# Diagonal term of stages 4 to 7 by GpSimd, the spread of w by two matmuls side by side, and the prologue listed anew

## The chip, the core and the metric

The kernel runs on one core of a Trainium2 chip. A core has TensorE (PE; weight loads are shown apart as PEld), VectorE (DVE), ScalarE (ACT), GpSimd (POOL) and SyncE (SP), and 16 DMA engines that serve the queues of POOL, ACT and SP. The metric is the device time of one execution in microseconds (us), lower being better. The kernel before takes 170.57 us, the median of 3 runs from 170.1 to 171.39.

## What is computed

A linear attention with a decaying state, whose result goes through two matrix products with a leaky ReLU between them. The inputs r, k, v have 4 batches, 8 heads, 768 tokens and 48 channels a head; w and u have one value per head and channel.

```python
for t in range(S):
    cur = np.einsum('bhd,bhe->bhde', u[None] * kt, vt)
    y[:, :, t] = np.einsum('bhd,bhde->bhe', rt, state + cur)
    state = w[None, :, :, None] * state + np.einsum('bhd,bhe->bhde', kt, vt)
...
x = attn_out.transpose(0, 2, 1, 3).reshape(B * S, H * D)   # 3072 x 384
h = x @ w_in                                               # 384 x 2048
out = np.maximum(0.01 * h, h) @ w_out                      # 2048 x 384
```

The diagonal term is `cur`: what a token's own k and v give to its own y. For head h it is v of the token times the sum over the channels of r, u and k.

## The kernel before

The 768 tokens of each batch are cut into 6 chunks of 128; the 24 pairs of chunk and batch are called stages, numbered chunk first, so that stages 0 to 3 are the first chunk of the four batches, and stage n continues the state of stage n-4. For one stage:

- P (`prep_half`, L344, VectorE): r and k are multiplied by tables of powers of w (qtab, ktab), which gives q and k scaled to the middle of the chunk, in the tile qk. They need the loads of r and k.
- T and t (`turn_mm`, L398, and `turn_out`): qk is turned (channels to partitions) by four matmuls with the identity, and copied from PSUM into tp. Stages 0 to 7 do it so; from stage 8 on, X (`turn_dma`, L349) does it by a DMA transpose on the queue of SP.
- A (`a_mm`, L423): eight matmuls, two per pair of heads, of 48 rows each, alternately on the upper and lower rows of the array, give the scores of token against token in two PSUM banks.
- M (`a_mask_half`, halves a and b): VectorE brings the scores into the tile at, with the strict triangle alone.
- The diagonal term, in one of two ways. For n < DIAG: X (`diag`, L359) multiplies the turned q and k, D (`diag_mm`, L451) sums them over channels with the weights w u by four matmuls of two columns, Q (`scaled_v`, L366) multiplies v by the sums, and Y begins with three matmuls of the identity (L550) that put it into PSUM; M is a product with the mask (L432). For n >= DIAG: q (`row_sums`, L373, L375, L377, VectorE) computes k u, r k u and its sum over channels from the loaded r and k; Q (`diag_tile`, L384, GpSimd, two instructions) writes the identity times these sums into at; M is a predicated copy (L436) that writes the scores over it where the mask is set, and Y needs no further matmul.
- Y (`y_mm`, L557): the state and the scores against v, in strips of 32 columns: 16 small matmuls for stages 0 to 3, 28 for others. y (`y_out`, L571, ScalarE) copies the sum into xT.
- K and S (`kv_mm`, L464, and `state`): k transposed times v, and the new state: for stages from 4 on a sum (L525) and a product (L527).
- G, g or J, j (`g1`, L596, one stage with one group of 512 columns of w_in; `g1_pair`, L619, two stages with 256 columns; ScalarE's leaky ReLU behind each) and H, h (`g2`, L643, output copy L655, output DMA L657).
- r, k, v, wi, wo are loads on the queue of GpSimd (L222, L232, L236), in the order listed; r0 and k0 alone go by SP and ACT.
- F (`fill`, L260): matmuls of ones into a free bank, whose result nothing reads; the number is how many, of 256 columns each.

The order of the work up to stage 5's outputs is a written list, ORDER (L27 to L38), of such tokens with their stage. Every engine executes its part of the list in that order; semaphore waits come from which tile an operation reads and writes. After the list a regular loop (L696) over pairs of stages follows, from the pair 6 and 7 on: first matmuls of the pair, row sums and diagonal tiles of the pair after it, loads three pairs ahead, second matmuls, scores, Y, masks, states. The last of the list on TensorE are Y7, A9 and A8.

The tables come from w in the beginning: w is loaded as a row on one partition, spread over 128 partitions by a matmul with a row of ones (`spread_w`, L295, half of the channels at a time, in float32), its logarithm taken (lnw, L301) and the powers by an exponential (L306), each in halves A and B. Cm, Wl, C and W make columns of w and w u for the state and the diagonal sums; u16, U and utab spread u.

## Time and profile before

| | |
|---|---|
| median of 3 runs | 170.57 us |
| profiled execution | 170.54 us |
| its span, first to last instruction | 168.8 us |
| TensorE busy | 164.0 us, 97% of the span |
| VectorE, ScalarE, GpSimd busy | 107.6, 92.5, 103.8 us |
| share of the chain that ended last on TensorE | 96% |
| of it second matmuls (L643), first matmuls of pairs (L619) | 37%, 31% |
| fills (L260), 26 matmuls | 6.8 us busy, 2% of the chain |
| diagonal products on GpSimd (L384), 32 | 35.0 us, 1.12 each |
| GpSimd's queue (software DMA) | 10.03 MB in 76512 packets |

A line of a timeline has the start in us from the beginning of the span, the time from the start of the first to the end of the last of the instructions that it joins, the engine, the line of the kernel, the operation, what it writes and reads, and their number; in brackets the idle time before it and what ended that. Matmuls overlap their neighbours, so the difference of two starts tells what one costs, and it is less than the time shown. POOL's DMA lines are the issuing; the data lands some microseconds later.

### The profile page before, as it was taken

How to read it: one execution, taken by the hardware profiler on the slowest of the kernel's cores; microseconds unless marked ns; L12 is line 12 of the kernel's file. 1: busy time of each engine (PE TensorE's matmuls, PEld its weight loads, DVE VectorE, ACT ScalarE, POOL GpSimd, SP SyncE). 2: the span in 40 equal slices, each digit the busy share in tenths (PEclk: the TensorE clock that was granted, in tenths of full speed). 3: DMA queues.
4: the chain of work that ended last, by engine and by line, in shares of the span. 5: the costliest groups of instructions: out<-in, count | busy, mean ns of one | idle time of the engine just before them, and what ended most of it. 6: DMA issues, size and time to landing. Idle time of an engine off the chain costs nothing.

```text
span 168.8 us, 4933 instructions
## 1 busy us (share of the span) xinstructions
PE 164.0 (97%) x2127; PEld 124.4 (74%) x2127; DVE 107.6 (64%) x215; ACT 92.5 (55%) x172; POOL 103.8 (61%) x117
## 2 busy tenths in 40 slices
PE   5999999899999999999999999999999999999994
PEld 3577899798667867867867867768768668668663
DVE  7379989884376999999859959969866050000000
ACT  3855899587123933933834835735637538449221
POOL 7999999990059979897993993993707200000000
PEclk9999999999999999999999999999999999999999
DMA  6999999999999999969999299299941011011022
GB/s 106 155 170 133 163 163 173 185 190 149 110 177 144 161 62 153 193 82 169 126 140 171 55 143 177 65 109 131 147 122 50 0 50 47 0 50 47 25 74 93
DMA packets 99146, 19.67 MB, mean 117 GB/s; under 512 B 92338, under 2 KB 99124, under 8 KB 99124
## 3 DMA queue, kind: packets, MB, share of 16 engines
q0 software_dynamic: 76512, 10.03, 93.1%
q1 hardware_dynamic: 21554, 9.12, 25.2%
q8 instruction: 17, 0.28, 0.6%
q10 hardware_dynamic: 1058, 0.20, 0.6%
q14 instruction: 5, 0.04, 0.1%
HBM read 20.45 MB, written 4.72 MB: 149 GB/s over the span
## 4 chain that ended last, share of the span: by engine, by line
PE 96%; DVE 1%; issue 1%; ACT 0%; DVEq 0%
PE ps L643 37%; PE ps L619 31%; PE ps L596 6%; PE ps L557 6%; PE ps L423 4%; PE ps L260 2%; PE ps L464 2%; PE ps L398 2%; PE ps L295 1%; PE ps L550 1%; DVE v_sb L280 1%; PE ps L451 1%; PE ps L321 0%; DVE qk L344 0%; ACT out_sb L655 0%
## 5 line engine op out<-in xcount | busy, mean ns | idle before, releaser
L643 PE MATMUL ps<-w_out_sb,gT 128*128 128x384 bf16 (+2 forms) x400 | 65.7, 320 | 0.0
L619 PE MATMUL ps<-xT,w_in_sb 128*128 128x256 bf16 x480 | 54.3, 273 | 0.0
L643 PEld LDWEIGHTS ps<-w_out_sb,gT 128*128 128x128 bf16 x400 | 37.9, 98 | 22.1
L619 PEld LDWEIGHTS ps<-xT,w_in_sb 128*128 128x128 bf16 x480 | 46.7, 98 | 6.5 <-ACT xT L571 0.2
L384 POOL TENSOR_TENSOR at<-ident,s_tok 128x512 bf16<-128x512 bf16 x32 | 35.0, 1121 | 26.8 <-DVE s_tok L377 26.8
L629 ACT ACTIVATE gT<-ps 128x512 bf16<-128x512 f32 x80 | 47.8, 597 | 6.2 <-PE ps L619 1.3
L655 ACT ACTIVATE out_sb<-ps 128x384 f32<-128x384 f32 (+2 forms) x25 | 11.9, 477 | 52.9 <-PE ps L643 52.9
L436 DVE CAST_PREDICATED at<-mask,ps 128x512 bf16<-128x512 uint16 x32 | 19.9, 684 | 15.5 <-PE ps L423 15.5
L222 POOL DMA_DIRECT2D v_sb<-in_v_dram x24 | 22.5, 953 | 0.0
L222 POOL DMA_DIRECT2D k_sb<-in_k_dram x23 | 21.6, 947 | 0.0
L222 POOL DMA_DIRECT2D r_sb<-in_r_dram x23 | 21.1, 943 | 0.0
L571 ACT ACTIVATE xT<-ps 128x384 bf16<-128x384 f32 x24 | 11.0, 492 | 6.5 <-PE ps L557 6.5
L344 DVE TENSOR_TENSOR qk<-r_sb,qtab 128x384 bf16<-128x384 bf16 x23 | 13.4, 592 | 1.9 <-DMA r_sb<-in_r_dram 1.9
L344 DVE TENSOR_TENSOR qk<-k_sb,ktab 128x384 bf16<-128x384 bf16 x23 | 13.9, 606 | 0.0
L375 DVE TENSOR_TENSOR rku<-r_sb,ku 128x384 bf16<-128x384 bf16 x16 | 12.7, 794 | 0.5
L525 DVE TENSOR_TENSOR sum_t<-ps,st 128x384 bf16<-128x384 f32 x16 | 8.8, 550 | 5.2 <-PE ps L464 5.2
L596 PE MATMUL ps<-xT,w_in_sb 128*128 128x128 bf16 x192 | 12.0, 219 | 0.0
L557 PE MATMUL ps<-at,v_sb 128*32 128x128 bf16 x384 | 11.1, 219 | 0.6 <-issue 0.6
L432 DVE TENSOR_TENSOR at<-ps,mask 128x512 bf16<-128x512 f32 x16 | 10.5, 682 | 0.9 <-PE ps L423 0.9
L606 ACT ACTIVATE gT<-ps 128x512 bf16<-128x512 f32 x16 | 9.6, 600 | 2.7 <-PE ps L596 2.1
L596 PEld LDWEIGHTS ps<-xT,w_in_sb 128*128 128x128 bf16 x192 | 10.9, 98 | 0.1
L557 PEld LDWEIGHTS ps<-at,v_sb 128*32 128x32 bf16 x384 | 8.7, 97 | 1.1 <-issue 0.7
(60 smaller groups left out, 131.7 us busy)
## 6 DMA issues: line engine op xcount, KB each, us to landing
out_dram<-out_sb SPq DMA_DIRECT2D x23, 192.0 KB, 3.9
v_sb<-in_v_dram POOLq DMA_DIRECT2D x24, 96.0 KB, 6.0
r_sb<-in_r_dram POOLq DMA_DIRECT2D x23, 96.0 KB, 5.6
k_sb<-in_k_dram POOLq DMA_DIRECT2D x23, 96.0 KB, 5.1
w_in_sb<-in_moe_w_in_dram POOLq DMA_DIRECT2D x4, 384.0 KB, 5.6
w_out_sb<-in_moe_w_out_dram POOLq DMA_DIRECT2D x4, 384.0 KB, 7.9
tp<-qk SPq DMA_TRANSPOSE x16, 4.6
k_f<-in_k_dram ACTq DMA_DIRECT2D x1, 192.0 KB, 2.8
```

The costliest lines, as they stand in the source:

```text
L222: add("pool", lambda: G.dma_start(dst, src), R=pace, W=[(which, n)], dma=f"{which}{n}")
L344: add("dve", lambda: V.tensor_tensor(qk[iq][:, H * half:H * half + H, 0:D], hd(src), hd(tab[:, :]), ALU.mult), R=[(name, n), ("qk"[half] + ...
L375: add("dve", lambda: V.tensor_tensor(rku[i2][:, :], r_of(n), ku[i2][:, :], ALU.mult), R=[("r", n), ("ku", i2)], W=[("rku", i2)])
L384: add("pool", lambda hh=hh, s_of=s_of: G.tensor_tensor(at[ia][:, hh, :, :], ident[:, :].unsqueeze(1).to_broadcast([128, NP, 128]), s_of.un ...
L436: add("dve", lambda: V.copy_predicated(at[n % NAT][:, hh, :, :], mask[:, :].bitcast(mybir.dt.uint16).unsqueeze(1).to_broadcast([128, NP, 1 ...
L557: last = PE.matmul(ps_y[32 * q:32 * q + 32, 128 * s:128 * s + 128], a, m, start=not whole and step == 0, stop=step == len(columns[q]) - 1)
L571: add("act", lambda: A.activation(xT[m % NX][:, :, 128 * half:128 * half + 128], ps_y[:, 0:HD].rearrange("p (s t) -> p s t", t=128), AF.Copy),
L596: last = PE.matmul(ps_g[:, 128 * f:128 * f + 128], w_in_sb[:, s, 128 * fb:128 * fb + 128], xT[ix][:, s, t], start=s == 0, stop=s == NSL - 1)
L619: last = PE.matmul(ps_g[:, 256 * f:256 * f + 256], w_in_sb[:, s, 128 * fb:128 * fb + 128], xT[ix][:, s, :], start=s == 0, stop=s == NSL - 1)
L629: add("act", lambda: A.activation(gT[ig][:, 2 * j:2 * j + 2, :].rearrange("p f t -> p (f t)"), ps_g[:, :], AF.Prelu, alpha=0.01), R=[key], ...
L643: last = PE.matmul(ps_o[:, 0:c1 - c0], gT[ig][:, s, 128 * half:128 * half + 128], w_out_sb[:, s, c0:c1], start=s == 0, stop=s == NFB - 1)
L655: add("act", lambda: A.activation(out_sb[io][:, c0:c1], ps_o[:, 0:c1 - c0], AF.Copy), R=[key], W=held)
```

## The change

DIAG goes from 8 to 4. So stages 4 to 7 take the second way for the diagonal term: row sums on VectorE, the diagonal tile by two products on GpSimd for each stage, and a predicated copy for the mask; their X, D and the three matmuls of Y with the identity are gone.

w is loaded as two rows of 192, on partitions 0 and 64, and spread by two matmuls, one on each partition, into two neighbouring PSUM banks; logarithm and tables are then one instruction of 384 columns each instead of two of 192. For that the eight banks become one tensor, and one_row has 128 partitions. u8 and u are loaded by SP instead of ACT. A fill has 128 columns instead of 256.

The whole list is written anew. Among the moves: the memsets of qk stand ahead of ones; r2 is GpSimd's first load and wi1 the second; stage 2's q is made first; fills are 76 of 128 columns in 21 places instead of 26 of 256 in 9; Q4 and Q5 stand after the load of k6, Q7, Q6, Q9 and Q8 among and behind the last loads; the transposes of stages 9 and 8 (X9T, X8T) come after P9q and P8q, and the list ends on TensorE with K9, Y7, Y6, A9, A8. On VectorE the last part reads S8, M7b, M7a, M6b, S7, P10k, M6a, S9, P11k, M9a. Lines of the changed kernel are 1 to 9 higher than before: L353 is `prep_half`, L393 the diagonal product, L441 and L445 the two forms of the mask, L559 and L566 those of Y.

```diff
--- before.py
+++ after.py
@@ -23,18 +23,18 @@
 NSL = HD // 128
 
 FIRST, NB, PACE = 6, B, 3
-TURNED, DIAG, CARRY, EXACT = 8, 8, 4, 1
+TURNED, DIAG, CARRY, EXACT = 8, 4, 4, 1
 ORDER = """
-w k0 r0 u8 w8 u ones tcol wi0 v0z r2 table exps one id wlz qk0 F6 bcA r1 id8 F2 bcB lnA k1 u16 wu8 ktabA F1 Cm k2 lnB U
-qtabA ktabB v0 utab P0k qtabB Wl wi3 F6 T0k P0q W C tri t0k@ F1 T0q v1 P1q t0q P2q F6 T1q X0 r3 A0 P1k t1q T2q M0a T1k
-k3 t2q D0 P2k F1 K0 t1k Q0 T2k v2 M0b t2k F1 A1 X1 v5 F2 Y0 X2 M1b A2 k4 y0 D2 M1a D1 K1 G0.0 k5 Q1 M2b G0.3 g0.0 wi1
-P3q Y1 P3k g0.3 r4 S1 T3q y1 K2 Q2 T3k t3q v3 G1.3 S2 t3k M2a G1.0 r5 g1.3 P4k Y2 X3 g1.0 r8 P5k A3 S0 y2 K5 M3b r6 T5k
-G2.3 t5k S5 k7 G2.0 g2.3 M3a G1.1 k9 g2.0 P4q G0.1 g1.1 wi2 T4k g0.1 D3 P5q K3 r7 T4q Q3 t4k T5q G2.1 S3 t5q k6 P8q Y3
-t4q P6q X5 A5 v4 g2.1 P7k A4 X4 y3 D5 T6q M4a wo3 T7k t6q G3.0 M5a v8 t7k G3.3 Q5 g3.0 wo0 M5b D4 G3.1 g3.3 P9k k8 G2.2
-M4b g3.1 P7q G1.2 wo2 g2.2 P6k T7q v6 g1.2 T6k t7q@ K4 Y5 t6k Q4 wo1 A7 y5 X6 A6 k11 S4 Y4 M7b v9 D6 y4 G3.2 M6a v10
-J2.4 M6b g3.2 J2.3 M7a v11 j2.4 J2.5 X7 j2.3 r10 D7 J2.1 j2.5 q8 r9 J2.2 j2.1 J2.6 r11 j2.2 P8k J2.0 j2.6 v7 X8T K8 Q6
-K6 j2.0 G0.2 k10 S6 Y6 g0.2 S8 J2.7 y6 H1 j2.7 P11k K9 H2 h1 S9 P10q H0 h2 P9q q9 X9T P11q K7 Q9 H3 Q7 h0 X11T S7 P10k
-X10T Q8 Y7 h3 A9 y7 A8 M9a M8a M9b M8b k12 r12 v12 k13 r13 v13
+w k0 r0 w8 u8 u qk0 r2 table ones wi1 one v0z id F12 bc tcol r1 exps id8 wlz lnw k3 qtab wu8 v0 F10 Cm u16 P2q ktab P0q
+F2 U r3 T2q Wl P0k utab T0q k1 C t2q T0k t0q k2 t0k@ W P1q tri F9 A0 X0 wi3 P3k F1 T1q M0b v3 F3 K0 M0a t1q F2 T3k F3
+D0 wi2 P3q t3k S0 F6 T3q v2 Q0 t3q P2k F12 Y0 P1k k4 X3 A3 y0 F1 T1k r5 M3b F1 D3 T2k t1k G0.1 M3a t2k v1 G0.3 X1 g0.1
+Q3 r4 D1 K3 X2 g0.3 A1 S3 F1 A2 r7 Y3 M1a F1 D2 M1b k5 y3 F3 G0.2 M2a G3.3 wo0 g0.2 Q2 G3.1 wi0 P4k g3.3 M2b T4k g3.1
+G3.2 v5 P5q t4k Q1 K1 T5q wo3 g3.2 Y2 S1 P4q t5q Y1 v4 q4 y2 F2 T4q y1 v10 F2 G2.1 t4q G1.2 k6 g2.1 P5k P7q G2.2 g1.2
+q5 Q4 T5k g2.2 G1.1 t5k T7q G2.3 g1.1 t7q Q5 A5 F1 A4 g2.3 G3.0 M4a F1 G1.0 M4b g3.0 K5 wo1 G0.0 M5a g1.0 r6 M5b G2.0
+g0.0 S5 K2 k9 Y5 g2.0 S2 F1 Y4 y5 k7 K4 y4 F2 G1.3 S4 wo2 J2.4 g1.3 P6k r9 J2.7 j2.4 T6k r10 j2.7 J2.6 t6k J2.3 q6 v7
+j2.6 J2.1 j2.3 k8 J2.0 j2.1 v11 P9k J2.2 P7k j2.0 P6q T7k r8 q7 j2.2 J2.5 t7k T6q v8 H1 j2.5 t6q r11 q9 v6 k10 P10q A7
+h1 P8k A6 P9q H2 Q7 X9T q8 v9 P11q K8 H3 h2 P8q Q6 S8 X8T M7b M7a k11 K6 M6b K7 h3 H0 Q9 S7 P10k Q8 M6a K9 X10T Y7 h0
+S9 Y6 y7 A9 y6 A8 P11k M9a X11T M9b M8b M8a S6 k12 r12 v12 k13 r13 v13
 """
 
 
@@ -148,9 +148,9 @@
     r_sb = SB("r_sb", [128, NST, HD])
     k_sb = SB("k_sb", [128, NST, HD])
     v_sb = SB("v_sb", [128, NST, H * E])
-    w_row = SB("w_row", [1, HD], FP32)
+    w_row = SB("w_row", [128, HD // 2], FP32)
     u_row = SB("u_row", [1, HD], FP32)
-    one_row = SB("one_row", [1, 128], FP32)
+    one_row = SB("one_row", [128, 128], FP32)
     u_row16 = SB("u_row16", [1, HD])
     w_head = SB("w_head", [H, D], FP32)
     u_head = SB("u_head", [H, D], FP32)
@@ -169,7 +169,7 @@
     kexp = SB("kexp", [128, 1], FP32)
     wcol = SB("wcol", [128, NP], FP32)
     wl = SB("wl", [128, NP, 2 * D])
-    ones = SB("ones", [128, 256])
+    ones = SB("ones", [128, 128])
     mask = SB("mask", [128, 128])
     ident = SB("ident", [128, 128])
     ku = [SB(f"ku{i}", [128, HD]) for i in range(4)]
@@ -184,7 +184,8 @@
     xT = [SB(f"xT{i}", [128, NSL, 256]) for i in range(NX)]
     gT = [SB(f"gT{i}", [128, NFB, 256]) for i in range(NG)]
     out_sb = [SB(f"out_sb{i}", [128, HD], FP32) for i in range(NO)]
-    ps = [ctx.enter_context(nc.psum_tensor(f"ps{i}", [128, 512], FP32)) for i in range(8)]
+    ps_all = ctx.enter_context(nc.psum_tensor("ps", [128, 8, 512], FP32))
+    ps = [ps_all[:, i, :] for i in range(8)]
 
     V, A, PE, SP, G = nc.vector, nc.scalar, nc.tensor, nc.sync, nc.gpsimd
     sch = Sched(ctx, nc)
@@ -257,7 +258,7 @@
 
         def emit():
             for _ in range(n):
-                last = PE.matmul(ps[i][:, 0:256], ones[:, 0:128], ones[:, 0:256], start=True, stop=True)
+                last = PE.matmul(ps[i][:, 0:128], ones[:, :], ones[:, :], start=True, stop=True)
             return last
 
         add("pe", emit, R=["ones"], W=[("ps", i), f"fill{n}"])
@@ -287,24 +288,32 @@
         add("dve", lambda: V.memset(wl[:, :, :], 0.0), W=["wl"])
         add("dve", lambda: V.memset(wu[:, :, :], 0.0), W=["wu"])
 
-    half_bank = {}
-
-    def spread_w(half):
-        ps_w, key = half_bank[half] = take()
-        cols = slice(192 * half, 192 * half + 192)
-        add("pe", lambda: PE.matmul(ps_w[:, cols], one_row[:, :], w_row[:, cols], start=True, stop=True),
-            R=["one_row", "w_row"], W=[key])
-
-    def log_w(half):
-        ps_w, key = half_bank[half]
-        cols = slice(192 * half, 192 * half + 192)
-        add("act", lambda: A.activation(lnw[:, cols], ps_w[:, cols], AF.Ln), R=[key], W=[("lnw", half)])
-        give(key)
-
-    def table(dst, exps, name, half):
-        cols = slice(192 * half, 192 * half + 192)
-        add("act", lambda: A.activation(dst[:, cols], lnw[:, cols], AF.Exp, scale=exps[:, 0:1]),
-            R=[("lnw", half), name + "exp"], W=[(name + "tab", half)])
+    w_bank = []
+
+    def spread_w():
+        for half in range(2):
+            w_bank.append(take())
+        assert w_bank[1][1][1] == w_bank[0][1][1] + 1
+
+        def emit():
+            for half in range(2):
+                at0 = slice(64 * half, 64 * half + 1)
+                last = PE.matmul(w_bank[half][0][:, 0:192], one_row[at0, :], w_row[at0, :], start=True, stop=True)
+            return last
+
+        add("pe", emit, R=["one_row", "w_row"], W=[w_bank[0][1], w_bank[1][1]])
+
+    def log_w():
+        i = w_bank[0][1][1]
+        add("act", lambda: A.activation(lnw[:, :].rearrange("p (two c) -> p two c", two=2),
+                                        ps_all[:, i:i + 2, 0:192], AF.Ln),
+            R=[w_bank[0][1], w_bank[1][1]], W=["lnw"])
+        give(w_bank[0][1])
+        give(w_bank[1][1])
+
+    def table(dst, exps, name):
+        add("act", lambda: A.activation(dst[:, :], lnw[:, :], AF.Exp, scale=exps[:, 0:1]),
+            R=["lnw", name + "exp"], W=[name + "tab"])
 
     def small_identity():
         add("dve", lambda: V.tensor_copy(ident8[:, :], ident[0:H, 0:H]), R=["ident"], W=["ident8"])
@@ -342,7 +351,7 @@
         iq = n % NQK
         src, tab, name, done = ((r_of(n), qtab, "r", "qp"), (k_of(n), ktab, "k", "kp"))[half]
         add("dve", lambda: V.tensor_tensor(qk[iq][:, H * half:H * half + H, 0:D], hd(src), hd(tab[:, :]), ALU.mult),
-            R=[(name, n), ("qk"[half] + "tab", 0), ("qk"[half] + "tab", 1), ("qk0", iq)], W=[(done, iq)])
+            R=[(name, n), "qk"[half] + "tab", ("qk0", iq)], W=[(done, iq)])
 
     def turn_dma(n):
         iq = n % NQK
@@ -659,16 +668,16 @@
 
     half_of = {"q": 0, "k": 1, "a": 0, "b": 1}
     single = {
-        "w": lambda: add("sp", lambda: SP.dma_start(w_row[:, :], row(w)), W=["w_row"], dma="w"),
+        "w": lambda: add("sp", lambda: SP.dma_start(
+            w_row[0:65:64, :], dram(w, 0, [[HD // 2, 2], [1, HD // 2]])),
+            W=["w_row"], dma="w"),
         "w8": lambda: add("sp", lambda: SP.dma_start(w_head[:, :], by_head(w)), W=["w_head"], dma="w8"),
-        "u8": lambda: add("act", lambda: A.dma_start(u_head[:, :], by_head(u)), W=["u_head"], dma="u8"),
-        "u": lambda: add("act", lambda: A.dma_start(u_row[:, :], row(u)), W=["u_row"], dma="u"),
+        "u8": lambda: add("sp", lambda: SP.dma_start(u_head[:, :], by_head(u)), W=["u_head"], dma="u8"),
+        "u": lambda: add("sp", lambda: SP.dma_start(u_row[:, :], row(u)), W=["u_row"], dma="u"),
         "one": lambda: add("dve", lambda: V.memset(one_row[:, :], 1.0), W=["one_row"]),
         "tcol": tokens, "ones": filled, "exps": exponents, "v0z": zero_v, "qk0": zero_qk, "wlz": zero_w,
         "id": identity, "tri": triangle, "table": preload, "id8": small_identity, "wu8": wu_product,
-        "bcA": lambda: spread_w(0), "bcB": lambda: spread_w(1), "lnA": lambda: log_w(0), "lnB": lambda: log_w(1),
-        "qtabA": lambda: table(qtab, qexp, "q", 0), "qtabB": lambda: table(qtab, qexp, "q", 1),
-        "ktabA": lambda: table(ktab, kexp, "k", 0), "ktabB": lambda: table(ktab, kexp, "k", 1),
+        "bc": spread_w, "lnw": log_w, "qtab": lambda: table(qtab, qexp, "q"), "ktab": lambda: table(ktab, kexp, "k"),
         "Cm": columns_mm, "Wl": log_columns, "C": decay_columns, "W": decay_table,
         "u16": u_cast, "U": u_spread, "utab": u_table,
     }
```

## The prediction

> **What bounds the kernel now.** I read the page first, then the chain that ended last, then the timelines of each engine up to 63 us.
>
> ```profile
> span 168.8 us, 4933 instructions
> PE 164.0 (97%) x2127; PEld 124.4 (74%) x2127; DVE 107.6 (64%) x215; ACT 92.5 (55%) x172; POOL 103.8 (61%) x117
> PE 96%; DVE 1%; issue 1%; ACT 0%; DVEq 0%
> ```
>
> The chain is TensorE nearly from end to end. From 53.52 us on, where the written list ends and the regular loop begins, both kernels do the same work in the same order. So the question is when the loop's first pair of matmuls (L619) can start, and whether its feeding engines are late by then. In the trace of before:
>
> ```profile
> 9.03 1.49 PE L260 MATMUL ps<-ones 128*128 128x256 bf16 x6
> 12.61 0.40 PE L398 MATMUL ps<-ident,qk 128*128 128x128 bf16 x4 [0.18 <-DVE qk L344]
> 31.94 0.23 PE L557 MATMUL ps<-at,v_sb 128*32 128x128 bf16 x2 [0.56 <-issue]
> 53.52 5.41 PE L619 MATMUL ps<-xT,w_in_sb 128*128 128x256 bf16 x48
> ```
>
> Between 12.8 and 53.5 TensorE pauses once, for 0.56 us at 31.4, with no releaser. Everything else is work. The other engines have room late in the prologue: GpSimd waits 10.22 us before stage 9's diagonal tiles, and VectorE is busy 5.31 of the 10 us from 40 to 50.
>
> The rows that decide this change are VectorE's and GpSimd's when both work on SBUF:
>
> ```profile
> 48.53 4.28 POOL L384 TENSOR_TENSOR at<-ident,s_tok 128x512 bf16<-128x512 bf16 x4 [10.22 <-DVE s_tok L377]
> 47.43 0.36 DVE L375 TENSOR_TENSOR rku<-r_sb,ku 128x384 bf16<-128x384 bf16 x1
> 50.71 1.19 DVE L344 TENSOR_TENSOR qk<-k_sb,ktab 128x384 bf16<-128x384 bf16 x1
> 57.39 2.97 DVE L375 TENSOR_TENSOR rku<-r_sb,ku 128x384 bf16<-128x384 bf16 x1
> 69.38 1.08 DVE L375 TENSOR_TENSOR rku<-r_sb,ku 128x384 bf16<-128x384 bf16 x1
> ```
>
> A VectorE product of two SBUF tiles takes 0.35 us alone; one that meets a GpSimd diagonal product (1.05 each) ends 0.2 us after that product ends. Products that read PSUM (L366 at 48.55, L525 at 49.69) keep their 0.55 beside the same tiles.
>
> **Part by part.** All terms are against the profiled execution: 170.54 us, a span of 168.8 and 1.74 around it; the median of the runs is 170.57. I laid the two lists out engine by engine, each instruction starting when its engine is free and what it waits for has ended, with start-to-start durations from the rows. For before this gives 52.7 for the loop's first matmul; the trace has 53.52, of which 0.56 is the pause without releaser.
>
> *TensorE's own work.* In before, from the first turning matmul (7.96) to 53.52, the rows give: turning 4.5, A 3.3, D 1.0, K 2.05, Y 6.3, first matmuls 10.7 and 5.25, second 10.4, fills 2.1, together 45.6. Removed: four groups D of 0.105, 0.4; three 128-column matmuls (L550) in each of Y4 to Y7, whose groups go from 0.77 to the 0.45 of the loop's Y, 1.3. The pause and short waits before D, A and K, some 1.4 with it, need not recur. Added: fills after that point are 52 of 128 columns, 18 at 0.107 and 34 at 0.056, 3.8 in place of 2.1. The first turning matmul moves to 6.6 (next part). So 6.6 + 45.6 - 0.4 - 1.3 - 1.4 + 1.7 gives 50.8: 2.7 us early if nothing waits.
>
> *The start.* ones and one_row come behind six memsets of 0.14, so the fills begin at 2.0 instead of 1.25, end at 3.3 and cover nothing that was needed before. The spread of w: each half took 0.92 (L295); side by side I take 0.92 for both, at most 1.84. Nearest row: A's eight matmuls of 48 rows, alternating between upper and lower rows, take 0.26, 33 ns each, against 56 ns in turning. Then log 0.49 and one table of 384 columns instead of two of 192 (0.35 to 0.45 each; I take 0.60, bounds 0.44 and 0.9), u's cast 0.43, the second table 0.60: ktab ends at 6.65, stage 0's k product at 7.24, its turn at 8.04. qtab alone, at 5.4, releases stage 2's q, whose load is now first on POOL's queue (5.1). w8, u8 and u now all queue behind r0 on SP; by w8's row (1.67 to 4.56) they land at 4.6, 5.1 and 5.6, and the cast of u waits 0.1.
>
> *VectorE.* The first masks move from 11.6 to 9.6. From 8.1 on it is never long idle: 12.2 us of products up to stage 4's row sums and 1.1 of waits puts these at 21.3. Per stage 4 to 7 it loses prod 0.33 and scaled v 0.46, and gains ku, rku and the reduction, 1.25 with their own waits; the masks stay at 0.60 as predicated copies (0.598 in the rows). That is +0.45 each, 1.8 in all, and it is hidden only while TensorE is not waiting for VectorE.
>
> *GpSimd and its queue.* Eight diagonal products of 1.05, 8.4 us, now stand inside the load list. Stage 4's run at 23.0 to 25.1, and stage 5's product rku meets them, so s of stage 5 is ready at 25.9. Stage 5's run to 28.1. Behind them are queued wo1, r6, k9, k7, wo2, r9, r10, v7, k8, v11, r8, v8, r11, v6, k10, v9 and k11 (15 at 0.87, 2 at 0.745) and the products of stages 7, 6, 9 and 8 (8 at 1.05): 23.0 us without a wait, to 51.1. In before the last load, k10, was issued at 37.20. The loads were landing some 8 us behind issue at 23 us, so of the 5.1 us pause only about 1 us reaches the queue.
>
> *The new wait.* Stages 9 and 8 occupy GpSimd from 46.8 to 51.1, and VectorE's list there reads S8, M7b, M7a, M6b, S7, P10k, M6a. S7's second product and P10k read two SBUF tiles and are held until 50.2 and 51.2; M6a runs behind P10k, to 51.9. Y6 on TensorE needs M6a; without the wait it would start at 49.9. So it waits 2.0, behind it queue A9, A8 and the loop, and the loop starts at 53.1, 0.4 earlier than in before. If one product slips between two tiles, M6a is earlier by 1.05. I take 0.5 for the gain: **170.0 us**.
>
> No row shows a predicated copy beside a diagonal product. The nearest rows are L366 and L525, unheld, and L344, held. I take unheld; held, M6b and M6a end up to 1 us later. The Trainium skill, GPSIMD Engine Reference, section 1 (Specifications), says that GpSimd shares its SBUF interfaces with those VectorE instructions that run in a 2-port mode or read two SBUF inputs; the copy reads one from PSUM, so by that page nothing is added and the loop starts at 53.1, and if the mask as input counted it would be about 54.
>
> *The clock.* Fills of 256 columns take 0.213 us each up to 10.5, while the loop's L619 (256 columns) takes 0.109; the page's clock row is 9 throughout. The turn comes at about 11.1, 4.4 us after unbroken matmuls began at 6.71. In after these begin at 6.6, so I leave it at 11. With the turn anywhere before 10.5 the layout gives 52.2; with 6.6 us of them instead of 4.4, at 13.2, it gives 54.5. The Trainium skill, TensorE: Matmul & The Clock Gate, Part 1, says that the full clock is released after a busy window of about 3.4 us which runs free of the kernel's start; by it the turn differs from run to run, within 10.0 and 13.4 (an estimate from that page), in both kernels alike.
>
> **Rivals.**
> - *The wait does not come* (faster): Y6 finds M6a done, because the products fall between the tiles or the loads land 0.4 us earlier and VectorE is past P10k in time. For it: the quanta are 1.05 us and the layout's error is of that size. Against: GpSimd's 23 us have no gap to slip. The loop starts at 50.8 to 51.4: 167.8 to 168.4.
> - *The last loads and transposes come late* (slower). K9 on TensorE needs v9, issued at 43.0 instead of 31.1; A8 needs stage 8's transpose, issued at 46.2, since it waits for P8q. In before a transpose took this long amid loads, and 2.7 us (47.83 to 50.57) without:
>
> ```profile
> 37.06 1.33 SPq L349 DMA_TRANSPOSE tp<-qk  x1
> ```
>
> It landed at 45.38, 8.3 us on. In after the loads are not through at 46. A8 is wanted at 52.6, so a landing after 6.4 us decides; at 8.3 (54.5) or issued 0.8 later behind the output on SP (55.3) the loop starts at 55.0 to 55.8: 172.0 to 172.8.
> - *The side-by-side matmuls run one after the other*: 0.92 later at the start, and by the layout 0.5 at the loop: 170.5. The parts removed from TensorE's list are gone in the list itself; there is no other way for the change not to do what it says.
>
> **How the numbers follow.** A difference of 1%, 1.7 us, is about what a measurement of this kernel can tell from none: its runs span 170.1 to 171.39. Forecast, with a wait at Y6 of 1 to 2.5 us and its variants of clock and spread (169.0 to 171.7): 0.58. No wait: 0.26. Late loads or transposes: 0.16. Faster by over 1% (under 168.9): 0.26; slower (over 172.3): 0.15; within: 0.59. Range: the no-wait case down to 168.0 and the late case up to 172.0; what lies outside is 0.1 on either side.
>
> **What would show it.** Right: Y6's group begins after a wait of 1 to 2 us released by VectorE's predicated copy (L445), P10k (L353) lasts about 1.2, GpSimd has no gap from 28 to 51, the masks of stage 0 (L441) start near 9.6, no L559 after stage 3. Wrong: TensorE reaches the loop before 51.5 with no wait; or waits at K9 or A8 with a DMA as releaser; or VectorE waits for loads (r6, r9, k8) by more than 2 us each; or the clock turns after 13 us.

## The result, and the profile after

The changed kernel takes 175.84 us (median of 6 runs, 175.66 to 177.01); the kernel before took 170.08 us beside it (6 runs, 169.36 to 171.39). The ratio is 1.036, with a 95% interval of 1.033 to 1.039: slower by 5.8 us, where 170.0 had been forecast, with a range of 168.0 to 172.0. The profiled execution took 175.8 us, with a span of 174.0.

The page of after, its head and its chain:

```profile
span 174.0 us, 4986 instructions
PE 165.0 (95%) x2149; PEld 125.9 (72%) x2149; DVE 115.7 (66%) x218; ACT 92.0 (53%) x170; POOL 111.9 (64%) x125
...
PEclk9999999999969999999999999999999999999999
...
PE 69%; POOL 10%; DVE 9%; DMA 7%; issue 3%; ACT 0%; POOLq 0%
```

Before, 96% of the chain was TensorE; now 26% belongs to GpSimd, VectorE and transfers. TensorE's timeline from 46 us on (the lines of Y, one each for a few matmuls, are left out) says where:

```profile
48.04 0.48 PE L473 MATMUL ps<-v_sb,qk 128*128 128x96 bf16 x4 [2.05 <-DVE qk L353]
48.31 4.30 PE L652 MATMUL ps<-w_out_sb,gT 128*128 128x384 bf16 x16
...
53.59 2.77 PE L652 MATMUL ps<-w_out_sb,gT 128*128 128x384 bf16 x16 [0.64 <-DVE sum_t L534]
...
57.50 0.24 PE L566 MATMUL ps<-tp,st 128*32 128x128 bf16 x4 [0.46 <-DVE at L445]
...
58.76 5.40 PE L628 MATMUL ps<-xT,w_in_sb 128*128 128x256 bf16 x48
```

The loop's first matmul (last line) starts at 58.76 us; before it was 53.52. That is +5.24 of the +5.26 between the two profiled executions, so all of the loss is made in the written list, and each wait shown has VectorE as its releaser. VectorE's timeline:

```profile
42.59 5.30 DVE L353 TENSOR_TENSOR qk<-k_sb,ktab 128x384 bf16<-128x384 bf16 x1
...
49.32 3.74 DVE L353 TENSOR_TENSOR qk<-r_sb,qtab 128x384 bf16<-128x384 bf16 x2
52.99 0.55 DVE L534 TENSOR_TENSOR sum_t<-ps,st 128x384 bf16<-128x384 f32 x1
```

and GpSimd's beside it:

```profile
41.71 1.00 POOL L223 DMA_DIRECT2D k_sb<-in_k_dram  x1
42.60 2.18 POOL L393 TENSOR_TENSOR at<-ident,s_tok 128x512 bf16<-128x512 bf16 x2
44.60 1.00 POOL L223 DMA_DIRECT2D v_sb<-in_v_dram  x1
45.55 2.11 POOL L393 TENSOR_TENSOR at<-ident,s_tok 128x512 bf16<-128x512 bf16 x2
47.55 0.94 POOL L223 DMA_DIRECT2D k_sb<-in_k_dram  x1
48.51 4.34 POOL L393 TENSOR_TENSOR at<-ident,s_tok 128x512 bf16<-128x512 bf16 x4
```

P8k, stage 8's k product, takes 0.35 us alone. Here it starts at 42.59 and ends at 47.89, after Q7's two products, a load issue and Q6's two. P11q takes 2.62 and P8q 1.19 beside Q9 and Q8 (together the 3.74). Their excess over 0.35 is 4.95 + 2.27 + 0.84 = 8.1 us. P8q ends at 53.07; from there VectorE works without a pause through S8, M7b, M7a, M6b, S7 and P10k to M6a, which ends at 57.45 and releases Y6.

So the first theory, **T1**: the loss is this long hold, which the prediction had taken to end with the one product that is met. The rivals: **T2**, GpSimd's load queue is late, because 8.4 us of products stand among its issues; **T3**, the start is late (Cm began at 6.61 instead of 5.85 us) and that carries to the end. For T2 there is one sign in the profile, which the prediction had named: VectorE waits 2.17 us for r6, which lands at 36.93. But P8k began at 42.59 all the same, 3.4 us before K8 came up on TensorE, and behind 17 us no wait of TensorE ends with a load.

### The profile page after: what moved, and what is told of

Read it like the earlier page. It is cut to its first block, busy times and chain, and to the rows that moved or that the text cites. A ratio compares the mean times of both kernels' runs of the same rounds, so it can differ in the third digit from the quotient of the medians.

```text
span 174.0 us, 4986 instructions
## 1 busy us (share of the span) xinstructions
PE 165.0 (95%) x2149; PEld 125.9 (72%) x2149; DVE 115.7 (66%) x218; ACT 92.0 (53%) x170; POOL 111.9 (64%) x125
## 4 chain that ended last, share of the span: by engine, by line
PE 69%; POOL 10%; DVE 9%; DMA 7%; issue 3%; ACT 0%; POOLq 0%
PE ps L652 30%; PE ps L628 27%; PE ps L566 5%; DVE qk L353 4%; DMA v_sb<-in_v_dram 4%; DMA k_sb<-in_k_dram 3%; POOL r_sb L223 3%; PE ps L432 3%; POOL k_sb L223 3%; PE ps L473 2%; PE ps L605 2%; DVE at L445 1%; POOL at L393 1%; DVE ku L382 1%; POOL v_sb L223 1%
## 5 line engine op out<-in xcount | busy, mean ns | idle before, releaser
L652 PE MATMUL ps<-w_out_sb,gT 128*128 128x384 bf16 (+2 forms) x400 | 67.5, 325 | 0.7 <-DVE sum_t L534 0.6
L393 POOL TENSOR_TENSOR at<-ident,s_tok 128x512 bf16<-128x512 bf16 x40 | 43.7, 1121 | 23.8 <-DVE s_tok L386 23.8
L445 DVE CAST_PREDICATED at<-mask,ps 128x512 bf16<-128x512 uint16 x40 | 24.9, 683 | 15.7 <-PE ps L432 15.7
L353 DVE TENSOR_TENSOR qk<-r_sb,qtab 128x384 bf16<-128x384 bf16 x23 | 18.0, 786 | 1.0 <-DMA r_sb<-in_r_dram 1.0
L353 DVE TENSOR_TENSOR qk<-k_sb,ktab 128x384 bf16<-128x384 bf16 x23 | 17.9, 784 | 0.1
L386 DVE TENSOR_REDUCE s_tok<-rku 128x8 f32<-128x384 bf16 x20 | 11.1, 553 | 0.7
L261 PE MATMUL ps<-ones 128*128 128x128 bf16 x76 | 9.4, 260 | 2.0 <-DVE ones L251 2.0
L605 PEld LDWEIGHTS ps<-xT,w_in_sb 128*128 128x128 bf16 x192 | 11.1, 98 | 0.1
L566 PE MATMUL ps<-at,v_sb 128*32 128x128 bf16 x384 | 10.8, 220 | 0.0
L566 PE MATMUL ps<-tp,st 128*32 128x128 bf16 x240 | 9.3, 221 | 0.5 <-DVE at L445 0.5
```

The lines of the kernel that those rows point to most:

```text
L353: add("dve", lambda: V.tensor_tensor(qk[iq][:, H * half:H * half + H, 0:D], hd(src), hd(tab[:, :]), ALU.mult), R=[(name, n), "qk"[half] + ...
L386: add("dve", lambda: V.tensor_reduce(s_tok[i2][:, :], hd(rku[i2][:, :]), AX.X, ALU.add), R=[("rku", i2)], W=[("s", i2)])
L393: add("pool", lambda hh=hh, s_of=s_of: G.tensor_tensor(at[ia][:, hh, :, :], ident[:, :].unsqueeze(1).to_broadcast([128, NP, 128]), s_of.un ...
L445: add("dve", lambda: V.copy_predicated(at[n % NAT][:, hh, :, :], mask[:, :].bitcast(mybir.dt.uint16).unsqueeze(1).to_broadcast([128, NP, 1 ...
L566: last = PE.matmul(ps_y[32 * q:32 * q + 32, 128 * s:128 * s + 128], a, m, start=not whole and step == 0, stop=step == len(columns[q]) - 1)
L605: last = PE.matmul(ps_g[:, 128 * f:128 * f + 128], w_in_sb[:, s, 128 * fb:128 * fb + 128], xT[ix][:, s, t], start=s == 0, stop=s == NSL - 1)
```

## Experiments: the hold against the late loads

**Loads ahead of the products.** Only GpSimd's order differs.

```diff
-q9 v6 k10 P10q A7 h1 P8k A6 P9q H2 Q7 X9T q8 v9 P11q ... M7a k11 K6
+q9 v6 k10 v9 k11 P10q A7 h1 P8k A6 P9q H2 Q7 X9T q8 P11q ... M7a K6
```

> The changed kernel, with GpSimd's loads v9 and k11 moved ahead of the diagonal products of stages 7, 6, 9 and 8 (only GpSimd's order differs). T1 (the loss is VectorE's product of stage 8, L353, which began 10 ns before Q7's first product and was held 5.30 us through four of them, plus the 1.5 us that the next second matmuls lost at a lower clock): that product takes about 0.35 us, K8 on TensorE does not wait 2 us, the next sixteen second matmuls take 2.76 us instead of 4.30, the loop's first matmul starts at 53.5 to 55.5 instead of 58.76, and the time is 171 to 173 us. T2 (loads are late because GpSimd's products stand among them): two loads come 2 us earlier, of which neither was waited for, so 175 to 176.5 us. T3 (the late start of 1.2 us carries to the end): no change, 175.8.

Measured: median 177.8 us of four runs, 174.57 to 178.61. The fastest lies below the changed kernel's 175.66, so whether the edit costs time these four don't tell. The profile is of the slowest, and in it the hold did not go, it grew. VectorE and then GpSimd:

```profile
41.36 9.48 DVE L353 TENSOR_TENSOR qk<-r_sb,qtab 128x384 bf16<-128x384 bf16 x1
```

```profile
40.95 0.99 POOL L223 DMA_DIRECT2D v_sb<-in_v_dram  x1
41.82 1.00 POOL L223 DMA_DIRECT2D k_sb<-in_k_dram  x1
42.69 1.01 POOL L223 DMA_DIRECT2D v_sb<-in_v_dram  x1
43.55 1.02 POOL L223 DMA_DIRECT2D k_sb<-in_k_dram  x1
44.45 6.17 POOL L393 TENSOR_TENSOR at<-ident,s_tok 128x512 bf16<-128x512 bf16 x6
52.70 2.21 POOL L393 TENSOR_TENSOR at<-ident,s_tok 128x512 bf16<-128x512 bf16 x2 [2.09 <-DVE s_tok L386]
```

Stage 10's q product begins inside a load issue and is held through three more issues and six products. It ends 0.22 us after the sixth, when GpSimd stops because it needs s of stage 8, which is queued behind the held product on VectorE. My expectation of 171 to 173 us failed: I had put the blame on the 10 ns between P8k and Q7. The near coincidence is not what makes the hold, and to have the loads issued earlier did not remove it.

**The tiles on VectorE.** In `diag_tile`, for the stages of the list:

```diff
+            eng, on = ("dve", V) if n < 10 else ("pool", G)
-            add("pool", lambda ...: G.tensor_tensor(
+            add(eng, lambda ...: on.tensor_tensor(
```

> The changed kernel, with the diagonal tiles of stages 4 to 9 written by VectorE instead of GpSimd (Q9 and Q8 put behind M6a; the tiles inside the loop stay on GpSimd). No GpSimd product is left before the loop, so no VectorE product can be held there; VectorE gets 12 more products of some 0.55 us, 6.6 us in all, 4.4 of them between 42 and 56 us. T1: no L353 above 0.4 us before 55 us, K8 without a wait of 2 us, the loop starts at 52 to 54.5, 169.5 to 172 us. T2: the loads come up to 8.4 us earlier too, 170 to 173. T3: the late start remains and VectorE is later still, 175 to 177.

Measured: 174.43 us, ratio 1.023 (1.014 to 1.033), above the expectation; the loop starts at 55.72. No VectorE product before the loop is held, and TensorE has no wait between Cm and A8. Then:

```profile
52.37 0.40 PE L433 MATMUL ps<-tp 48*128 48x128 bf16 x8
55.38 0.40 PE L433 MATMUL ps<-tp 48*128 48x128 bf16 x8 [2.62 <-DMA tp<-qk]
55.72 7.08 PE L629 MATMUL ps<-xT,w_in_sb 128*128 128x256 bf16 x48
```

Without that wait A8 would start at 52.76. Stage 8's transpose was issued at 46.63 and landed at 55.25, 8.62 us on, and the 48 matmuls behind the wait took 7.08 us instead of 5.40. So T1 holds for the first obstacle, and the late transpose, which the prediction named as a rival, stands right behind it.

**The transpose too.** In addition to the edit above:

```diff
-X9T q8 v9 P11q K8 H3 h2 P8q Q6 S8 X8T M7b
+X9T q8 v9 P8q X8T P11q K8 H3 h2 Q6 S8 M7b
+    def behind(n):                     # loads of stages 12, 13
+        return [("tp", 8 % NTP, 0)] if n >= 12 else []
```

> The kernel with the diagonal tiles of the list on VectorE, with two more edits: stage 8's transpose is issued ahead of the output of stage 2 on SP, and the loads of stages 12 and 13 on GpSimd wait until that transpose has landed. Without the holds TensorE ran without a wait until 52.76 us and then waited 2.62 us at A8 for the transpose, which took 8.62 us from issue to landing beside those loads; the 48 first matmuls after the wait took 7.08 us instead of 5.41. If the late transposes are what is left of the loss: A8 waits less than 0.5 us, the first pair takes 5.41, the loop starts at 52.8 to 53.5 and the time is 169.8 to 170.8 us. If the transposes are slow for another reason: A8 still waits 2 us or more, 173 to 175.

Measured: 170.98 us, ratio 1.005 (1.003 to 1.008). The transpose lands 3.54 us after its issue (44.75 to 48.29), A8 does not wait, and the loop starts at 53.11. The time is 0.2 us above the expectation, for a wait of 0.61 in the loop's first pair, at a bank that VectorE's masks free. The two edits give back 4.86 of the 5.76 us.

**The transpose alone**, with the tiles on GpSimd as they were.

> The changed kernel with the edit on the transposes alone (stage 8's ahead of stage 2's output, loads of stages 12 and 13 behind it), tiles on GpSimd as they were. T1: the hold of stage 8's product at 42.6 us stays at about 5.3 us, K8 waits some 2 us, and the time is 175.2 to 176.2: the transposes are a second obstacle behind the first. If the transposes were the loss by themselves: 171.5 to 173.

Measured: 177.17 us, ratio 1.040 (1.036 to 1.044); the expectation was too low by 1 us, in T1's direction. This time stage 10's q product is held for 5.89 us (42.79 to 48.68), and K8 waits 2.55:

```profile
49.09 0.33 PE L473 MATMUL ps<-v_sb,qk 128*128 128x96 bf16 x4 [2.55 <-DVE qk L353]
54.52 4.45 PE L652 MATMUL ps<-w_out_sb,gT 128*128 128x384 bf16 x16 [2.15 <-DVE sum_t L534]
```

While a hold stands, the transposes bring nothing here; the hold itself was the longer one this time (5.89 instead of 5.30).

**Fills in the place of the wait.** Thirty fills ahead of K8 in the changed kernel (`P11q F30 K8 H3`).

> The changed kernel with 30 more fills of 128 columns (some 1.7 us) on TensorE just ahead of K8, where it waited 2.05 us. T1's part on the clock (the wait of 2.05 us made the next sixteen second matmuls take 4.30 us instead of 2.76): they take about 2.76, the loop starts 1.3 to 1.6 us earlier, at 57.2 to 57.5, 174.2 to 174.6 us. If the clock fell for another reason, H3 keeps its 4.3 us and the time is 175.6 to 176.

Measured: 176.82 us, ratio 1.039 (1.030 to 1.047): slower than the changed kernel, though the matmuls behind K8 kept their speed.

```profile
47.98 0.33 PE L473 MATMUL ps<-v_sb,qk 128*128 128x96 bf16 x4 [0.60 <-DVE qk L353]
48.15 2.76 PE L652 MATMUL ps<-w_out_sb,gT 128*128 128x384 bf16 x16
...
53.54 2.77 PE L652 MATMUL ps<-w_out_sb,gT 128*128 128x384 bf16 x16 [2.28 <-DVE sum_t L534]
```

H0, the last line, starts at 53.54, in the changed kernel at 53.59: the 1.54 us that H3 lost there to the clock were hidden, because H0 waits for VectorE anyway. I had counted them as part of the loss; that was wrong. The rest of the 1 us is a wait of 0.92 at A8 for the transpose.

**The diagonal part alone**, in the list of before: DIAG = 4, row sums and tiles where the products of the turned q and k stood.

> The kernel before with the diagonal part of the change alone: stages 4 to 7 by row sums, GpSimd's products and a predicated copy, in the list of before (row sums and tiles where the products of the turned q and k stood, 7's ahead of 6's); start, spread of w, fills and order otherwise as before. T1: GpSimd's products meet VectorE's at other places, one hold of some 0.8 us each unless one starts just before a run of them; with no long hold 169.5 to 171.5 us, with one 172 to 175, and the trace shows which instruction. T3: with the old start it is at most 171. If the diagonal part costs by itself whatever the order, 173 or more without a single hold above 1.3 us.

Measured: 178.60 us, ratio 1.045 (1.035 to 1.055). TensorE waits 0.98, 2.76, 1.03 and 2.69 us between 24 and 43. Part of it is a late load (VectorE waits 1.84 us for r5, which landed at 23.76, in before at 22.23), part my placement (the masks at 31.14 wait 1.79 us for GpSimd's tile), part T1 again: S's second product, L527, begins 0.23 us into a load issue and takes 2.88 us through Q6's two products. That it came out above the range tells that the list has to be made for the new term; it does not price the term.

## Experiments: the start

**The part on w alone**, in the list of before.

> The kernel before with the part on w alone: w as two rows, two matmuls side by side, logarithm and tables of 384 columns in one instruction each; list, fills and diagonal terms as before. By every theory it is no cause: the spread takes 0.94 instead of 0.92 twice, the tables 0.6 instead of twice 0.35 to 0.45, so P0k may start up to 1 us earlier and the loop at most 0.5: 169.3 to 170.6 us. If this part costs something that the trace of the changed kernel hides, 171 or more.

Measured: 173.05 us, ratio 1.017 (1.013 to 1.021). This was no theory's expectation. SyncE's queue in this kernel, and the TensorE line that waits:

```profile
0.80 0.67 SPq L671 DMA_DIRECT2D w_row<-in_w_dram  x1
1.52 0.43 SPq L214 DMA_DIRECT2D r_f<-in_r_dram  x1
2.01 0.46 SPq L674 DMA_DIRECT2D w_head<-in_w_dram  x1
```

```profile
7.95 0.34 PE L493 MATMUL ps<-ident,w_head 8*48 8x8 f32 x4 [2.96 <-DVE wu_head L322]
```

The load of w as two rows takes 0.67 us to issue instead of 0.33, so r0 is issued at 1.52 instead of 1.19. r0 landed at 7.65 instead of 4.29, 6.1 us after its issue instead of 3.1, and w by head, queued behind it, came with it. TensorE waits 2.96 us at Cm, and the loop starts at 55.51, 2.0 later than in before. The spread itself costs what I had said. That the longer issue is what made r0 late is not shown: the first of r0's 16 parts landed at 3.92, no later than in before (4.02), and the others came spread over 3.7 us. Other loads (k0 on ACT, wi0 on GpSimd) run at that time; none was moved to try it.

**The start alone**, in the changed kernel: `w k0 w8 r0 u8 u` instead of `w k0 r0 w8 u8 u`, u8 and u issued by ACT.

> The changed kernel with the edit on the start alone: w by head ahead of r0 on SP, u by head and u on ACT. T3 (the late start carries to the end): Cm 0.7 to 1.0 us earlier than 6.61, and the whole gain arrives, 174.8 to 175.2 us. T1: the loop waits for VectorE, whose holds are set by GpSimd's run between 42 and 53 us; that run moves by at most 0.5 us, so 175.2 to 176, unless the products now meet the run at another place, when a hold changes by 1 to 5 us.

Measured: 175.91 us, ratio 1.034 (1.031 to 1.038), the time of the changed kernel. Cm starts at 5.48, 1.13 us earlier, and nothing of it arrives: stage 10's q product is held from 41.26 to 47.15, and the loop starts at 58.45. T3 falls; while the hold stands, the start is worth nothing either.

**The same on the mended kernel.** First u8 and u by ACT alone (on top of the tiles on VectorE and the transpose):

> The one before (tiles on VectorE, transpose first, loads of stages 12 and 13 behind it) with u by head and u loaded by ACT again, as in the kernel before, instead of by SP behind r0 and w8. T3 (the start is late because these two land at 6.35 and 6.7 us): Cm on TensorE starts 0.6 to 1.0 us earlier than 6.61, and the loop starts 0.4 to 1.0 us earlier: 169 to 170.2 us, faster than before by up to 1 us. If the start is bound by the tables instead: Cm is earlier and the loop is not, the time is that of the run beside it.

Measured: 170.87 us, ratio 1.005 (1.003 to 1.008), as beside it. Cm was now waiting for w by head, not for u. Then w by head ahead of r0, and stage 9's and 8's tiles moved so that the masks free their banks in time:

```diff
-w k0 r0 w8 u8 u
+w k0 w8 r0 u8 u
-S7 P10k M6a K9 X10T Y7 h0 S9 Q9 Q8 Y6 y7 A9 y6 A8 P11k M9a X11T M9b M8b M8a
+S7 P10k M6a Q9 K9 X10T Y7 h0 S9 Y6 y7 A9 y6 A8 P11k M9a X11T M9b Q8 M8b M8a
```

> The kernel with the tiles on VectorE, the transpose first, the late loads behind it and u on ACT, with two more edits: w by head is loaded by SP ahead of r0 instead of behind it (it landed at 6.3 us behind r0, and TensorE waited 0.81 us for it), and stage 9's tile is made before S9, stage 8's behind the masks of stage 9 (the loop's first pair waited 0.61 us for a bank that these masks free). If the order of SP's queue makes the late start: Cm at 5.3 to 5.9 us instead of 6.36, the loop starts 0.3 to 0.8 us earlier, no wait in its first pair, 169.3 to 170.2 us against some 170.1 of before. If the loads landing late at the start are bound by the memory and not by the order: w by head still lands after 6 us, and 170.2 to 170.9.

Measured: 169.81 us, ratio 0.9985 (0.9967 to 1.0002). Cm starts at 5.47 and TensorE does not wait at all. Yet the loop starts at 52.60, as in the run before (52.63): the fills of 128 columns turn from 0.107 to 0.055 us at about 11.8 here and at about 10.9 there, so what the earlier start gave was spent at half clock. Of the 0.80 us between the two profiled executions the wait of 0.62 us in the first pair, now gone, is the larger part. From before this kernel can't be told.

**Without the late fills.** The 16 fills behind Y0 are taken out.

> The one before without the 16 fills that stand behind Y0 (1 to 3 of 128 columns each). In the run without holds and late transposes TensorE had no wait after 6.3 us, so these fills, some 1.0 us together, were paid in full if the work behind them was ready: 0.4 to 1.0 us less than the run beside it, 168.6 to 169.8, faster than before by up to 0.8%. If they covered waits, the time is the same as beside it and waits of VectorE's products appear at their places.

Measured: 169.03 us, ratio 0.993 (0.991 to 0.996), as expected and the fastest of all, 0.7% below before. The loop starts at 51.74, 0.86 earlier than in the run with the fills. Of that 0.36 was there ahead of Y0 already (12.79 instead of 13.15), where the clock turned at 10.4 us instead of 11.8; behind Y0 it is 0.50. The 16 fills are 0.9 us, and in their place a wait of 0.43 us for v came (at 16.30): they covered part of a wait, and only the rest was paid.

## Experiments: what makes a hold long

**A measurement by itself.** GpSimd runs diagonal products (T) and load issues (D); VectorE makes a reduction of varied length and then two products of two SBUF tiles.

> A measurement by itself: nothing of the reference is computed, the output is zeros. In 42 trials GpSimd makes a run of diagonal products (T, 128x512) and load issues (D), and VectorE, after a reduction of varied length, two products of 128x384 from two SBUF tiles; in the last six trials two predicated copies from PSUM instead. T1: a product that begins inside T ends some 0.2 us after that T or one later; one that begins in the D ahead of a run of T is held through several of them, 2 us and more; a predicated copy keeps 0.68 or less. Against T1: every product ends after the first T that it meets, at most 1.3 us, wherever it begins, and the holds of 5 us in the kernel have another cause.

In 12 runs of T from idle, each of the 24 products ends at the latest some 0.2 us after the T in which it begins, and takes 1.20 us at most. Behind load issues most do not: the first products of a trial took up to 5.74 us, through five T, though some were let in after 1.19 to 1.30 us beside a run that had begun 0.01 to 0.02 us after an issue. VectorE and GpSimd in one trial from idle (product at 29.43) and in one behind three load issues (product at 271.02):

```profile
29.43 1.48 DVE L164 TENSOR_TENSOR y_sb<-x_sb,tab 128x384 bf16<-128x384 bf16 x2
...
271.02 6.85 DVE L164 TENSOR_TENSOR y_sb<-x_sb,tab 128x384 bf16<-128x384 bf16 x2
...
287.97 1.28 DVE L169 CAST_PREDICATED atd<-mask,ps 128x512 bf16<-128x512 uint16 x2
```

```profile
28.54 5.27 POOL L150 TENSOR_TENSOR at<-ident,s_tok 128x512 bf16<-128x512 bf16 x5 [0.37 <-ACT tick L174]
...
268.79 2.70 POOL L160 DMA_DIRECT2D k_sb<-in_k_dram  x3 [0.69 <-ACT tick L174]
271.48 6.18 POOL L150 TENSOR_TENSOR at<-ident,s_tok 128x512 bf16<-128x512 bf16 x6
...
287.91 5.04 POOL L150 TENSOR_TENSOR at<-ident,s_tok 128x512 bf16<-128x512 bf16 x5 [0.53 <-ACT tick L174]
```

Each line joins the two products of its trial. At 271.02 the first of them takes the 5.74 us. The predicated copies (287.97) take 0.68 us each in all six trials beside T: they are not held, which the prediction had taken without a row.

**In the kernel.** The fastest kernel, with the tiles of stages 6 to 9 back on GpSimd behind all loads up to stage 11, once directly and once behind a wait for P8k:

```diff
-                R=["ident", ("s", n % 4)], W=[("at", ia, hh)])
+                R=["ident", ("s", n % 4)] + [("kp", 8 % NQK)] * (n == 7), W=[("at", ia, hh)])
```

> The fastest kernel so far (tiles of the list on VectorE, transposes and start mended, no late fills), with the tiles of stages 6 to 9 back on GpSimd: all loads up to stage 11 are issued first, and the products of stages 7, 6, 9 and 8 follow the last load issue directly. If a run of products that follows a load issue directly holds VectorE's products for several of its own: one hold of 2 us or more near 38 to 43 us, K8 waits 0.5 us or more, 170.5 to 174 us. If long holds come about otherwise: none above 1.3 us, 168.8 to 169.8.

> The one beside it with a single wait added: the run of GpSimd's products begins only when VectorE has made stage 8's k product (L353), so it starts from idle, some 2 to 3 us after the last load issue. If a run from idle lets a waiting product in at each boundary, as in the loop: every hold is 1.2 us or less, about six of them on VectorE, K8 does not wait, 168.8 to 170 us. If the number of products in the run decides: a hold of 2 us or more here too, and 170.5 us or more.

Measured: 171.01 us, ratio 1.004 (1.001 to 1.006), without the wait, and 169.67 us, ratio 0.997 (0.995 to 0.999), with it. The pair does not tell what it was meant to: without the wait GpSimd was through with its loads and stood 0.32 us for s of stage 7, so both runs began from idle, and in both no hold exceeds 1.23 us. (Without the wait Y6 waits 0.73 us for M6a.) What it does show is that products on GpSimd can stand in this place without a long hold. Eight of them back to back with the wait, GpSimd's line and VectorE's:

```profile
40.65 8.63 POOL L394 TENSOR_TENSOR at<-ident,s_tok 128x512 bf16<-128x512 bf16 x8 [2.62 <-DVE qk L353]
```

```profile
40.68 1.23 DVE L382 TENSOR_TENSOR ku<-k_sb,u_tab 128x384 bf16<-128x384 bf16 x1
41.94 1.08 DVE L384 TENSOR_TENSOR rku<-r_sb,ku 128x384 bf16<-128x384 bf16 x1
43.06 0.55 DVE L386 TENSOR_REDUCE s_tok<-rku 128x8 f32<-128x384 bf16 x1
43.53 1.73 DVE L353 TENSOR_TENSOR qk<-r_sb,qtab 128x384 bf16<-128x384 bf16 x2
```

**The candidates apart.** Again by itself, with one, two and four D, with eight T from idle, and with one D and a wait of 2.3 us.

> A measurement by itself again; nothing of the reference is computed, the output is zeros. 17 trials: runs of 5 to 7 diagonal products (T) directly behind one, two or four load issues (D), from idle, or behind one load issue and a wait of some 3 us; VectorE's two products begin at varied places. If the load issue directly ahead makes the hold long: behind D without a gap 2 us and more, from idle and behind the wait 1.2 us at most. If the number of load issues decides: long behind four and two, short behind one. If neither: long holds in the runs from idle as well.

VectorE and GpSimd in the second trial (one D, then T directly) and in one of the last three (one D, the wait, then T):

```profile
15.54 6.19 DVE L165 TENSOR_TENSOR y_sb<-x_sb,tab 128x384 bf16<-128x384 bf16 x2
...
135.24 2.31 DVE L165 TENSOR_TENSOR y_sb<-x_sb,tab 128x384 bf16<-128x384 bf16 x2
```

```profile
14.26 0.94 POOL L161 DMA_DIRECT2D k_sb<-in_k_dram  x1 [0.59 <-ACT tick L175]
15.21 6.03 POOL L151 TENSOR_TENSOR at<-ident,s_tok 128x512 bf16<-128x512 bf16 x6
...
130.93 0.94 POOL L161 DMA_DIRECT2D k_sb<-in_k_dram  x1 [0.70 <-ACT tick L175]
134.18 6.27 POOL L151 TENSOR_TENSOR at<-ident,s_tok 128x512 bf16<-128x512 bf16 x6 [2.31 <-ACT long_out L193]
```

One load issue directly ahead is enough: the first product takes 5.92 us, through the whole run of T. A product that began in the first T of a run took 4.95 behind two D and 4.97 behind four. From idle, in a run of eight, no product exceeds 1.19 us, and behind the wait none either. Neither the number of load issues nor the length of the run makes the hold long; it takes a load issue directly ahead of the run. In all traces together, 553 products of two SBUF tiles met T of a run from idle, and none took more than 1.23 us.

But not every run behind an issue holds a product long. The first trial did not follow: there T began 0.10 us after D had ended, and the hold was 0.88. Row sums in three of the kernels got in after 1.08 us, too, beside runs that began 0.01 to 0.04 us after an issue. Sorted by that gap, the traces show this much: where the first T began before the issue had ended, by 0.01 to 0.13 us (in the changed kernel T at 42.60, the issue's end at 42.71), the first product that had to wait for T was held for 2.97 to 9.48 us, in all 13 such runs; where it began 0.01 to 0.10 us after, the holds range from 1.08 to 5.92. That this overlap is a cause is not shown; no run sets it.

## Why the prediction was wrong, step by step

- **The hold, the step that failed.** "One that meets a diagonal product ends 0.2 us after that product ends." The rows I had read for it were runs that wait for the row sums, so from idle, and for those it is right (1.08 to 1.23). In the list the products stand directly behind load issues, and there the hold was 5.30 us instead of 1.2 (4.90 to 9.48 in its variants with these tiles on GpSimd). With these tiles on VectorE and the transpose earlier, 4.86 of the 5.76 us were gone. I quoted the row that showed it, L375 at 57.39 with 2.97 us, and passed it over: it begins inside a load issue, with two products directly behind. The queue without a gap, which I had forecast for GpSimd from 28 us on (it came, 29.8 to 52.85), was just the condition of it.
- **The new wait.** Forecast at Y6, 2.0 us; measured 2.05 at K8, 0.64 at H0 and 0.46 at Y6. P10k, which I had expected to be held, took 0.35: VectorE was so late that GpSimd had finished. The releasers were as said, the place was not.
- **The late transposes**, a rival with a chance of 0.16: not the cause, since X8T landed at 58.10 and A8 started at 58.24 without a wait. With the hold gone they cost 2.62 us and the clock behind it; the price of 172.0 to 172.8 was somewhat low against 174.43.
- **The other rivals.** TensorE did reach the loop without a wait once the holds, the transposes and w by head were mended, but at 52.60, not at 50.8: my sum of TensorE's own work was 1.8 us short. About 0.8 of it is the clock: at half clock the matmuls from the first turning on ran for 3.5 us in before (7.96 to about 11.5; eight score matmuls at 10.88 still take 0.61, so the prediction's reading of 11.1 for the turn was 0.4 too early) and for 5.1 in that kernel (6.73 to about 11.8). The other 1.0 is not worked out. The side-by-side matmuls take 0.94 us for both, as forecast.
- **The start.** The masks of stage 0 came at 10.79 instead of 9.6. I took the landing of w by head from its row in before, but with w as two rows r0 landed at 5.97 instead of 4.29, and with it all that queues behind it on SP. Why r0 was late stays open. It cost nothing here (175.91 us without it), and 2.0 us at the loop where it stood alone.
- **What was right.** No L559 after stage 3, the products of stages 4 and 5 held by one T each (P7q 1.20, ku 1.19), the copies not held, the loop equal in both.
- **The clock.** It turned at about 10.5 us, where 11 was taken; in the other kernels of this text it came between 9.4 (the diagonal part alone) and 13.8 (the transpose alone), so it differs from run to run. That it falls again behind a wait (H3 4.30 us) was not foreseen, and cost nothing there.

The hold speaks to a rule. The Trainium skill, SBUF — State Buffer, section "SBUF: two separate sides", says that the port pair that VectorE and GpSimd share goes to whichever starts first for the whole instruction and that the other is blocked till then. By that a hold ends with the running product, 1.2 us at most. This case agrees for runs from idle (1.23 at most) and disagrees in most runs directly behind a load issue (5.92 through six instructions).

## What to carry to other kernels

Before work is moved from TensorE to GpSimd, look at what stands directly ahead of it on GpSimd's queue: a run of products directly behind load issues held one of VectorE's two-tile products through three to six of them here, a run behind a wait through one at a time. Where there is room, give the work to VectorE itself (eight tiles of 0.62 us are 5.0 us, the one hold was 5.30) or make GpSimd wait before the run. And when one row of an operation is three times as long as the others, explain it before taking the others' number; it may be the only one that stands where the new code will.

## What the runs showed of the hardware

- A VectorE product of two SBUF tiles that met GpSimd products behind a load issue was held up to 9.48 us (from inside the load issue on), 27 times its 0.35; products that read PSUM (0.55) and predicated copies (0.68) ran beside products of GpSimd unchanged. What decides whether a boundary between two GpSimd products lets it in stays open: from idle and behind an issue alike, the next one begins a little before the former ends. P11q missed two boundaries and got in at the third (2.62 us, in the changed kernel and two variants) in a run that began 0.01 to 0.02 us after a load issue had ended.
- Load issues alone can hold a product too: 1.00 us for one that began 0.78 us into the first of two, 1.67 and 1.88 through three issues in the kernels of the transpose alone and of the start alone. In the kernel with the loads ahead, the product at 41.36 had stood 3.1 us when GpSimd's first product began.
- The granted clock fell behind some waits of TensorE and not behind others: after 2.05 us sixteen matmuls took 4.30 us instead of 2.76, after 2.62 the first pair 7.08 instead of 5.40, after 5.38 (loads ahead of the products) sixteen took 5.32; after 2.28 with thirty fills ahead, and after 2.55 and 2.15 in the run on the start, they took 2.76 and 2.77. The granted clock of the traces sorts them: it is halved for whole steps of 3.41 us (48.01 to 51.42 in the changed kernel), whose place differs from run to run. It was halved behind a step in which TensorE stood idle for 2.03 us or more (2.03 in the changed kernel, busy 1.38 of the 3.41 us from 44.60 on; 2.15 and 2.60 in the kernels of the transpose alone and of the tiles on VectorE) and stayed full behind one with 1.96 or less (1.96 in the run on the start, 1.41 with the thirty fills); a wait that two steps share counts in each by its part.
- TensorE's first turn to the full clock did not come sooner where its work began sooner: at about 11.8 us with Cm at 5.47, at about 10.9 with Cm at 6.36.
